# A recurrence, an attention mixture and a feed-forward block: norm's root on GpSimd, decay on ScalarE, mask as a VectorE copy

## The chip, the cores and the metric

The kernel runs on one core of one Trainium2 chip. The metric is device time in microseconds (us), the median over several executions. The core's engines run side by side, each with its own queue of instructions in a fixed order: TensorE (PE; its weight loads are PEld), VectorE (DVE), ScalarE (ACT), GpSimd (POOL) and SyncE (SP), which issues the transfers. An instruction waits until what it needs is done, and everything behind it in its queue waits with it.

## The reference

Three steps follow each other, each on the result of the one before. Sizes: 4 sequences (b), 768 steps, 8 heads of 48 columns (384 together), 4 experts of width 64, a feed-forward width of 1536.

```python
# 1. recurrence over time, a 48x48 state for each of 8 heads
for t in range(S):
    cur = einsum('bhd,bhe->bhde', u[None] * kt, vt)
    y[:, :, t] = einsum('bhd,bhde->bhe', rt, state + cur)
    state = wt[:, :, :, None] * state + einsum('bhd,bhe->bhde', kt, vt)
# 2. four causal attention experts, of which each row takes its top 2
logits = x @ w_gate; w = softmax over the top 2
q = x @ wq[e]; k = x @ wk[e]; v = x @ wv[e]
a = softmax(where(causal, -1e9, scale * (q @ k.T)))
out += mask * w * (a @ v @ wo[e])
# 3. norm and feed-forward, with the input added
xn = (x - mu) / sqrt(var + 1e-06) * g_ln
return x + maximum(xn @ w_ch1, 0.0) @ w_ch2
```

## The kernel before, in words

**Recurrence.** It is cut into 24 chunks of 128 steps, six to a sequence; `rwkv_chunk(n)` builds the work of one. Time lies along the free axis, four pairs of heads side by side, so the tiles are 128x512. Two scans on VectorE multiply up the decays (`scan` writes bw, `forth` writes fw), from bw also come the whole decay of the chunk (`decay`) and `begin`. k times bw is k2 (VectorE, `mk_k2`), r times fw is rp (GpSimd, `mk_rp`). TensorE multiplies them for each head (`mm_a`, into two PSUM banks pa, one for the even and one for the odd heads). This product is wanted only where the time of k lies before that of r: `am_copy` copies a bank to SBUF on ScalarE, and `am_mask` sets the rest to zero on GpSimd. `mm_intra` multiplies the masked tile am with v. What earlier chunks left behind is the state, a 48x48 block for each head: `mk_dec` multiplies it on GpSimd with the chunk's decay and writes it into a block-diagonal tile dec (two heads on the diagonal, zeros beside them), `mm_inter` multiplies that with rp into the same bank py, `mm_d` makes what the chunk adds, and `state` adds it to dec on VectorE and writes it into one of two tiles. k times r times u, summed by head, is done token by token on GpSimd and VectorE (`mk_rk`, `mk_ruk`, `mk_cb`, `mk_cv`); `xsum` adds it to py.

**Attention.** `project(b)` splits a sequence's rows into a high and a low half in fp16, transposes them by DMA and makes q, k, v and the gate. `attend(b)` goes over six tiles of 128 rows and four experts: scores ps, the row's maximum on VectorE (`s_max`, mx), the exponential on ScalarE (ex), the probabilities' high half on ScalarE and low half on GpSimd (hl), a transposing DMA (pt), the product with v (po), and the output projection (px, `mm_o`), which needs the low half o16 of VectorE.

**Norm and feed-forward.** For every two row tiles, `norm(b, g)` makes 1/sqrt of the variance from a bit trick (`n_start`, three instructions) and three Newton steps (`n_step`, four instructions each), all on VectorE on 128x2 elements, then normalises (`n_xn`, xn), splits (`n_hi`, `n_lo`) and transposes. `mlp(b, g)` runs the two products (pm and pz). Their weights come as raw integers and are decoded in the front part of the program, on VectorE (w_f), ScalarE and GpSimd (w_w).

**What sets the order.** Nothing is written in program order. Each step is an `op` with its engine, an assumed duration, what it comes after, and the buffers that it takes and frees. `Plan.order` then runs a list scheduler while the program is built: on each engine, of the steps that could start about now, it takes the one with the smallest due value, plus a price for lateness:

```python
o.due = sum(PLACE.get(k, 0.0) * f for k, f in o.terms)
...
pick = min(((o.due + late * (s - first), o.idx, s, o) for s, o in starts if s <= first + look))
```

PLACE is a table of some 270 numbers, one for each chunk, tile, group and kind of step; the order is fixed with it. While TensorE has nothing real to do, until 208 us of the planner's own time, it gets filler products of 128x512 (`spin`, line 577), whose results nobody reads.

## Time and profile before

| | |
|---|---|
| median of 3 runs | 743.48 us (739.04 to 746.66) |
| the profiled execution | 737.19 us, its span 735.3 |
| TensorE busy | 679.3 us, 92% of the span, 103.3 of it filler |
| VectorE busy | 518.8 us, 71% |
| ScalarE busy | 368.2 us, 50% |
| GpSimd busy | 295.3 us, 40% |

The span is that of the trace, from the first to the last instruction; 1.9 us lie around it. An average over the span says little here, since the program begins with recurrence, decoding and attention and ends with feed-forward.

### The profile page before, as it was taken

What the parts mean: (1) busy time and instruction counts of PE and PEld (TensorE: products, weight loads), DVE (VectorE), ACT (ScalarE), POOL (GpSimd) and SP (SyncE); (2) the same over time, 40 slices, a digit from 0 to 9 for tenths busy, and PEclk for the clock granted to TensorE, in tenths of its full rate; (3) what the DMA queues carried; (4) which work ended last, traced back from release to release, by engine and by line L of the source; (5) the groups of instructions that cost most, each with busy time, mean ns of one, the idle gap of its engine ahead of it and who ended that gap; (6) DMA issues with size and microseconds to landing.
All of it is one profiled execution on the core that took longest, in us unless ns stands there. A gap on an engine that the chain in (4) does not pass through costs nothing.

```text
span 735.3 us, 15608 instructions
## 1 busy us (share of the span) xinstructions
PE 679.3 (92%) x5753; PEld 486.6 (66%) x5753; DVE 518.8 (71%) x1326; ACT 368.2 (50%) x991; POOL 295.3 (40%) x317
## 2 busy tenths in 40 slices
PE   7899879998979899988999999989999989999996
PEld 4565536645557567766757686767677667685773
DVE  5888688787688996868899487957655754475521
ACT  5533473445867463556647445644553452554210
POOL 7366465444846671366546015650330220223000
PEclk9999889999989999999999999999999999999999
DMA  7555556736556684547695448464555342355110
GB/s 248 172 176 169 177 135 175 242 92 152 128 114 120 175 187 116 113 102 194 150 204 108 107 104 179 85 122 95 105 100 121 73 72 66 70 87 105 29 43 26
DMA packets 174004, 92.60 MB, mean 126 GB/s; under 512 B 144608, under 2 KB 156640, under 8 KB 173920
## 3 DMA queue, kind: packets, MB, share of 16 engines
q1 hardware_dynamic: 173920, 91.53, 53.3%
q8 instruction: 47, 0.77, 0.4%
q14 instruction: 37, 0.30, 0.1%
HBM read 44.31 MB, written 4.72 MB: 67 GB/s over the span
## 4 chain that ended last, share of the span: by engine, by line
PE 35%; DVE 26%; DMA 12%; ACT 6%; issue 4%; POOL 3%; SPq 1%; POOLq 0%; ACTq 0%; DVEq 0%
PE pz L1252 9%; DMA pt<-hl 9%; PE pm L1219 8%; PE pq L862 5%; DVE mx L1019 4%; POOL hl L1044 3%; PE py L757 2%; ACT ex L1031 2%; PE pv L917 2%; DMA xT<-xs 2%; DVE mx L1021 2%; DVE hid L1234 2%; PE spin L577 2%; DVE bw L631 1%; DVE fw L643 1%
## 5 line engine op out<-in xcount | busy, mean ns | idle before, releaser
L1044 POOL TENSOR_TENSOR hl<-ex,hl 128x128 f16<-128x128 f32 (+5 forms) x96 | 103.9, 1086 | 250.9 <-ACT hl L1040 207.9
L1219 PE MATMUL pm<-xnT,w_w 128*128 128x256 f16 x1296 | 154.6, 273 | 2.0 <-DVE hid L1234 1.3
L1252 PE MATMUL pz<-w_w,hid 128*128 128x384 f16 x864 | 153.1, 327 | 1.4 <-DVE hid L1234 1.4
L1219 PEld LDWEIGHTS <-w_w 128*128 128x128 f16 x1296 | 123.7, 98 | 20.3 <-issue 1.7
L1252 PEld LDWEIGHTS <-hid 128*128 128x128 f16 x864 | 82.1, 98 | 50.3 <-issue 1.4
L1031 ACT ACTIVATE ex<-ps,bias,scales 128x512 f32<-128x512 f32 (+3 forms) x128 | 79.9, 627 | 65.2 <-DVE bias L1023 51.6
L577 PE MATMUL spin<-starts,ident 128*128 128x512 bf16 x395 | 103.3, 403 | 2.9 <-POOL ident masks.py:199 2.1
L1019 DVE TENSOR_REDUCE mx<-ps 128x1 f32<-128x512 f32 (+3 forms) x128 | 61.4, 500 | 30.3 <-PE ps L1009 23.0
L577 PEld LDWEIGHTS <-ident 128*128 128x128 bf16 x395 | 39.1, 104 | 45.4 <-issue 10.9
L1230 ACT ACTIVATE hid<-pm 128x512 f16<-128x512 f32 x72 | 42.7, 593 | 52.6 <-PE pm L1219 52.5
L1040 ACT ACTIVATE hl<-ex 128x128 f16<-128x128 f32 (+5 forms) x96 | 54.4, 572 | 28.1 <-DMA pt<-hl 25.3
L1234 DVE SCALAR_TENSOR_TENSOR hid<-pm,hid 128x512 f16<-128x512 f32 x72 | 49.1, 683 | 21.9 <-ACT hid L1230 21.8
L1064 PE MATMUL po<-vt,pt 128*128 128x64 f16 x1008 | 45.3, 194 | 18.1 <-DMA pt<-hl 17.8
L1064 PEld LDWEIGHTS <-pt 128*128 128x128 f16 x1008 | 39.6, 99 | 31.9 <-DMA pt<-hl 27.1
L724 POOL TENSOR_SCALAR_AFFINE_SELECT am<-am 128x512 f32<-128x512 f32 x48 | 36.1, 767 | 49.0 <-ACT am L719 48.9
L862 PE MATMUL pq<-xT,w_qk 128*128 128x384 f16 x288 | 48.9, 326 | 1.5 <-DVE qk L881 1.5
L757 PE MATMUL py<-seq,am 128*128 128x48 f32 x384 | 46.7, 275 | 2.1 <-POOL am L724 2.1
L757 PEld LDWEIGHTS py<-seq,am 128*128 128x128 f32 x384 | 46.1, 194 | 3.5 <-POOL am L724 2.2
L667 POOL TENSOR_TENSOR rp<-seq,fw 128x512 f32<-128x512 f32 x24 | 32.4, 1351 | 27.4 <-DVE fw L643 22.2
L1006 PE MATMUL ps<-kd,qs 128*128 128x512 f16 (+3 forms) x128 | 39.7, 312 | 3.5 <-ACT ex L1031 3.4
L862 PEld LDWEIGHTS <-w_qk 128*128 128x128 f16 x288 | 28.0, 98 | 19.7 <-issue 2.0
L1007 PE MATMUL ps<-low,qs 128*128 128x512 f16 (+3 forms) x128 | 37.6, 312 | 0.0
(182 smaller groups left out, 1141.6 us busy)
## 6 DMA issues: line engine op xcount, KB each, us to landing
seq<-in_seq_dram SPq DMA_DIRECT2D x48, 256.0 KB, 4.2
tok<-in_tok_dram SPq DMA_DIRECT2D x24, 384.0 KB, 3.6
w_raw<-in_w_dram SPq DMA_DIRECT2D x36, 256.0 KB, 3.0
seq<-in_seq_dram SPq DMA_DIRECT2D x24, 258.5 KB, 3.0
...
```

What stands on the lines that cost most here:

```text
L577: T.matmul(bank("m", "spin"), ident16, ballast, start=True, stop=True)
L757: T.matmul(t["py"][:, h * D : (h + 1) * D], t["am"][h % 2][:, h // 2, :], t["vt"][:, h * D : (h + 1) * D], start=(c == 0 and h == 0), stop ...
L862: T.matmul(h["pq", half][:, :384].rearrange("p (c t) -> p c t", t=P), wt["qk"][:, lw, kk, mt * P : (mt + 1) * P], t["xT"][:, 3 * half : 3 ...
L1019: V.tensor_reduce(out=mx[:, ip : ip + 1], in_=h["ps"][ip][:, : k1 - k0], axis=AX.X, op=OP.max)
L1031: A.activation(h["ex"][:, k0:k1], h["ps"][ip][:, : k1 - k0], AF.Exp, bias=h["bias"], scale=t["esc"], accum_out=r["sums"][:, e, ip : ip + 1])
L1040: A.activation(h["hl"][:, :W], h["ex"][:, :W], AF.Copy)
L1044: G.tensor_tensor(out=h["hl"][:, W : 2 * W], in0=h["ex"][:, :W], in1=h["hl"][:, :W], op=OP.subtract)
L1064: T.matmul(r["po"][:, e * HD : (e + 1) * HD], r["pt"][e][:, lp * (i + 1) + kb, :], t["vt"][:, kb, lv, e * HD : (e + 1) * HD], start=(e == ...
L1219: T.matmul(h["pm"][:, j * 256 : (j + 1) * 256].rearrange("p (c t) -> p c t", t=P), wt["w1"][:, lw, kk, f * P : (f + 1) * P], q["xnT"][:, : ...
L1230: A.activation(hid[fp][:, 0], h["pm"], AF.Relu)
L1234: V.scalar_tensor_tensor(out=hid[fp][:, 1], in0=h["pm"], scalar=0.0, in1=hid[fp][:, 0], op0=OP.max, op1=OP.subtract)
L1252: T.matmul(h["po"][:, :DM], hid[fp][:, lh, c0 : c0 + P], wt["w2"][:, lw, 2 * fp + j, :], start=(fp + j + i == 0), stop=(fp == NF // 2 - 1 ...
```

## The change

Three steps are done in another way, and the table of the order is new.

- **Mask.** The copy to SBUF and the masking become one VectorE instruction, a copy under a mask (`copy_predicated`, with the 0/1 tile `above`). It writes only where the mask is 1; elsewhere the target keeps the zeros that it was given at the start. So the two targets (`ams`) are now fixed tiles, one for the even and one for the odd heads, and no longer taken from a ring.
- **Decay.** `mk_dec` moves from GpSimd to ScalarE, as four scaled copies of 128x96, one for each pair of heads, from one of the two block-diagonal tiles (`decs`) into the other. The state lives in these tiles: `state` adds into the tile in place. It must therefore wait for `mm_inter`, which reads the same tile, and `mm_d` is queued behind `mm_inter`.
- **Norm.** In place of `n_start` and three `n_step` stand one VectorE instruction (variance plus 1e-6, divided by 64) and one GpSimd instruction, that to the power -0.5.
- **Order.** The numbers of PLACE are all new, with the entries of the dropped steps left out.

```diff
--- before.py
+++ after.py
@@ -36,58 +36,57 @@
 
 PRM = dict(LOOK=0.09, LATE=389.29, UNTIL=208.0, SPAN=9.92, LEAST=2.644, GAP=0.05, NPA=6, NSM=0, NWA=24, NK2=0)
 PLACE = {
-    ('av', 0, 0): 2115.89, ('av', 0, 1): -962.38, ('av', 0, 2): -717.4, ('av', 0, 3): 4212.33, ('av', 0, 4): -1403.95,
...
+    ('av', 0, 0): -1586.12, ('av', 0, 1): -4443.5, ('av', 0, 2): -4729.91, ('av', 0, 3): 1027.27,
...
 }
 
 
@@ -277,7 +276,7 @@
     pass
 
 
-SIZES = dict(seq=2, bw=1, fw=2, rp=2, k2=2, tok=1, cv=1, dec=2, am=2, k2t=1, xf=1, xT=1, xs=2, qs=1, kd=1, kl=1,
+SIZES = dict(seq=2, bw=1, fw=2, rp=2, k2=2, tok=1, cv=1, am=2, k2t=1, xf=1, xT=1, xs=2, qs=1, kd=1, kl=1,
              vt=1, ex=2, hl=2, pt=3, of=1, o16=2, oT=2, hid=9, x1=3, xnT=2, r=3, a=2, o=1, m=2)
 RW = 256
 
@@ -339,12 +338,19 @@
     G.memset(neg, 0.0)
     G.affine_select(out=neg, in_=neg, compare_op=OP.is_ge, fill=-(2.0 ** 100), base=0,
                     pattern=[[-1, P]], channel_multiplier=1)
+    above = const.tile([P, P], mybir.dt.int8, name="above")
+    G.memset(above, 1)
+    G.affine_select(out=above, in_=above, compare_op=OP.is_ge, fill=0, base=-1, pattern=[[1, P]], channel_multiplier=-1)
+    ams = [const.tile([P, NP, P], F32, name=f"am{j}") for j in range(2)]
+    for a in ams:
+        V.memset(a, 0.0)
     begin = const.tile([P, NP * CW], F32, name="begin")
     V.memset(begin, 0.0)
-    states = [const.tile([P, NP, D], F32, name=f"state{i}") for i in range(2)]
     decs = [const.tile([P, NP, 2 * D], F32, name=f"dec{i}") for i in range(2)]
     for t in decs:
         V.memset(t, 0.0)
+    half = const.tile([P, 2], F32, name="half")
+    G.memset(half, -0.5)
     tri = const.tile([P, E, E], F32, name="tri")
     V.memset(tri, 0.0)
     for e in range(1, E):
@@ -693,13 +699,10 @@
 
         mk_dec = None
         if c:
-            @op("G", 0.94, after=[forth, before.get("state")], take=[mine("dec")])
+            @op("A", 1.18, after=[forth, before.get("state")])
             def mk_dec():
-                t["dec"] = decs[(b * (NC - 1) + c) % 2]
-                for j in range(2):
-                    rows, cols = slice(64 * j, 64 * j + D), slice(j * D, (j + 1) * D)
-                    G.tensor_tensor(out=t["dec"][rows, :, cols], in0=states[(c - 1) % 2][rows],
-                                    in1=decay[rows, n, :, None].to_broadcast([D, NP, D]), op=OP.mult)
+                for hp in range(NP):
+                    A.activation(decs[c % 2][:, hp], decs[(c - 1) % 2][:, hp], AF.Copy, scale=decay[:, n, hp : hp + 1])
 
         @op("PE", 1.0, dense=0.64, after=[mk_k2, mk_rp], follow=[before.get("py")], take=[mine(ta, 0), mine(ta, 1)], free=[mine("k2"), mine("rp")])
         def mm_a():
@@ -710,22 +713,15 @@
                     T.matmul(t["pa"][j][:, hp * P : (hp + 1) * P], t["k2"][o : o + D, hp, :], t["rp"][o : o + D, hp, :],
                              start=True, stop=True)
 
-        t["am"] = [None, None]
         masked = []
         for j in range(2):
-            @op("A", 0.59, after=[mm_a], follow=[me["am"] if j else before.get("am")], take=[mine("am", j)], free=[mine(ta, j)])
+            @op("V", 0.69, after=[mm_a], follow=[me["am"] if j else before.get("am")], take=[mine("am", j)], free=[mine(ta, j)])
             def am_copy(j=j):
-                t["am"][j] = buf("am", [P, NP, P], F32, f"am_{nm}_{j}")
-                A.activation(t["am"][j].rearrange("p h t -> p (h t)"), t["pa"][j], AF.Copy)
-
-            @op("G", 0.64, after=[am_copy])
-            def am_mask(j=j):
-                a = t["am"][j]
-                G.affine_select(out=a, in_=a, compare_op=OP.is_ge, fill=0.0, base=-1,
-                                pattern=[[0, NP], [1, P]], channel_multiplier=-1)
+                V.copy_predicated(ams[j], above[:, None, :].to_broadcast([P, NP, P]),
+                                  t["pa"][j].rearrange("p (h t) -> p h t", t=P))
 
             me["am"] = am_copy
-            masked.append(am_mask)
+            masked.append(am_copy)
 
         if not last:
             @op("PE", 0.44, after=[mk_k2], follow=[before.get("d")], take=[mine("r", "pk")], free=[mine("k2")])
@@ -741,11 +737,11 @@
 
         mm_inter = mm_d = None
         if c:
-            @op("PE", 0.9, dense=0.7, after=[mk_rp, mk_dec], follow=[mm_a], take=[mine("r", "py")], free=[mine("rp"), mine("dec")])
+            @op("PE", 0.9, dense=0.7, after=[mk_rp, mk_dec], follow=[mm_a], take=[mine("r", "py")], free=[mine("rp")])
             def mm_inter():
                 t["py"] = bank("r", f"py_{nm}")
                 for hp in range(NP):
-                    T.matmul(t["py"][:, hp * 2 * D : (hp + 1) * 2 * D], t["rp"][:, hp, :], t["dec"][:, hp, :],
+                    T.matmul(t["py"][:, hp * 2 * D : (hp + 1) * 2 * D], t["rp"][:, hp, :], decs[c % 2][:, hp, :],
                              start=(hp == 0), stop=False, skip_group_check=True)
 
         @op("PE", 1.74, dense=0.37, after=masked + [load_v], follow=[mm_inter], take=[] if c else [mine("r", "py")],
@@ -754,12 +750,12 @@
             if c == 0:
                 t["py"] = bank("r", f"py_{nm}")
             for h in range(H):
-                T.matmul(t["py"][:, h * D : (h + 1) * D], t["am"][h % 2][:, h // 2, :], t["vt"][:, h * D : (h + 1) * D],
+                T.matmul(t["py"][:, h * D : (h + 1) * D], ams[h % 2][:, h // 2, :], t["vt"][:, h * D : (h + 1) * D],
                          start=(c == 0 and h == 0), stop=(h == H - 1), skip_group_check=True)
 
         state = None
         if not last:
-            @op("PE", 0.79, dense=0.73, after=[mk_k2t, load_v], follow=[before.get("py")], take=[mine("r", "pd")], free=[mine("k2t"), mine("seq")])
+            @op("PE", 0.79, dense=0.73, after=[mk_k2t, load_v], follow=[mm_inter, before.get("py")], take=[mine("r", "pd")], free=[mine("k2t"), mine("seq")])
             def mm_d():
                 t["pd"] = bank("r", f"pd_{nm}")
                 for hp in range(NP):
@@ -767,16 +763,16 @@
                              t["vt"][:, hp * 2 * D : (hp + 1) * 2 * D],
                              start=(hp == 0), stop=(hp == NP - 1), skip_group_check=True)
 
-            @op("V", 0.72, after=[mm_d, mk_dec, before.get("dec")], free=[mine("r", "pd")] + ([mine("dec")] if c else []))
+            @op("V", 0.72, after=[mm_d, mm_inter, before.get("dec")], free=[mine("r", "pd")])
             def state():
                 pdv = t["pd"][:, :DM].rearrange("p (h j e) -> p h j e", j=2, e=D)
                 for j in range(2):
                     rows, cols = slice(64 * j, 64 * j + D), slice(j * D, (j + 1) * D)
-                    dst = states[c % 2][rows]
+                    dst = decs[c % 2][rows, :, cols]
                     if c == 0:
                         V.tensor_copy(dst, pdv[rows, :, j])
                     else:
-                        V.tensor_tensor(out=dst, in0=t["dec"][rows, :, cols], in1=pdv[rows, :, j], op=OP.add)
+                        V.tensor_tensor(out=dst, in0=dst, in1=pdv[rows, :, j], op=OP.add)
 
         @op("V", 0.56, after=[mm_intra, mk_cv], follow=[before.get("xsum")], take=[] if c else [("xf", b)],
             free=[mine("r", "py")])
@@ -1145,29 +1141,16 @@
         nm = f"{b}_{g}"
         plan.at("n", b, g)
 
-        @op("V", 0.5, after=att[b]["x1"][-2:])
-        def n_start():
-            q["v"], q["y"], q["t"] = (small(f"rs_{k}", [P, 2], f"rs_{k}_{nm}", 4) for k in "vyt")
-            V.tensor_scalar(q["v"], q["mv"][:, :, 1], 1e-6, None, op0=OP.add)
-            V.tensor_scalar(q["y"].bitcast(I32), q["v"].bitcast(I32), 1, None, op0=OP.logical_shift_right)
-            V.tensor_scalar(q["y"].bitcast(I32), q["y"].bitcast(I32), -1, 0x5F3759DF, op0=OP.mult, op1=OP.add)
-
-        step = n_start
-        for it in range(3):
-            @op("V", 0.65, after=[step])
-            def n_step(it=it):
-                v, y, t = q["v"], q["y"], q["t"]
-                V.tensor_tensor(out=t, in0=y, in1=y, op=OP.mult)
-                V.tensor_tensor(out=t, in0=t, in1=v, op=OP.mult)
-                V.tensor_scalar(t, t, -0.5, 1.5, op0=OP.mult, op1=OP.add)
-                if it < 2:
-                    V.tensor_tensor(out=y, in0=y, in1=t, op=OP.mult)
-                else:
-                    V.scalar_tensor_tensor(out=y, in0=y, scalar=8.0, in1=t, op0=OP.mult, op1=OP.mult)
-
-            step = n_step
-
-        @op("V", 0.87, pair=True, after=[step], take=[("ex", ("n", b, g))])
+        @op("V", 0.17, pair=True, after=att[b]["x1"][-2:])
+        def n_var():
+            q["v"], q["y"] = (small(f"rs_{k}", [P, 2], f"rs_{k}_{nm}", 4) for k in "vy")
+            V.tensor_scalar(q["v"], q["mv"][:, :, 1], 1e-6, 1.0 / 64, op0=OP.add, op1=OP.mult)
+
+        @op("G", 0.4, after=[n_var])
+        def n_root():
+            G.tensor_tensor(out=q["y"], in0=q["v"], in1=half, op=OP.pow)
+
+        @op("V", 0.87, pair=True, after=[n_root], take=[("ex", ("n", b, g))])
         def n_xn():
             q["xn"] = buf("ex", [P, 2, DM], F32, f"xn_{nm}")
             for t in range(2):
@@ -1277,8 +1260,8 @@
         seqs, toks = (a.rearrange("(b c) p n -> b c p n", c=NC) for a in (seq, tok))
         pair = small("pair", [P, 2], "pair", 1)
         G.memset(pair, 0.0)
-        state = states[0]
-        G.memset(state, 0.0)
+        state = decs[0][:, :, :D]
+        G.memset(decs[0], 0.0)
         for j in range(2):
             G.memset(pair[64 * j : 64 * j + 64, j : j + 1], 1.0)
         xf[B] = (buf("xf", [P, NC, DM], F32, "xf_g"), small("xm", [P, NC], "xm_g", 2))
```

The order moves in many places. Three are shown; in a row stand the line, the operation, what is written and what is read (names end in sequence, tile or chunk, and a running number).

VectorE ahead of the first norm's normalisation (rs_ are the Newton tiles, bw_2_0 is the scan of a chunk of sequence 2, xn the normalised rows), before:

```order
L1153 TENSOR_SCALAR rs_y_0_0_2625<-rs_y_0_0_2625 128x2
L1160 TENSOR_TENSOR rs_t_0_0_2626<-rs_y_0_0_2625 128x2
...
L1162 TENSOR_SCALAR rs_t_0_0_2626<-rs_t_0_0_2626 128x2
L1166 SCALAR_TENSOR_TENSOR rs_y_0_0_2625<-rs_y_0_0_2625,rs_t_0_0_2626 128x2
L631 SCALAR_TENSOR_TENSOR bw_2_0_2660<-seq_2_0_2588,starts_69 128x516
L1174 TENSOR_SCALAR xn_0_0_2712<-x1_0_0_2408,mv_0_0_2409,rs_y_0_0_2625 128x384 x2
L1019 TENSOR_REDUCE mx_0_3_1_2716<-ps_0_3_1_0_2703 128x1
```

The same place now (scales_1 and s_x1 belong to sequence 1's projection, am0 and am1 are the masked copies of chunk 2_0):

```order
L1147 TENSOR_SCALAR rs_v_0_0_2667<-mv_0_0_2576 128x2
L637 SCALAR_TENSOR_TENSOR bw_2_1_2670<-seq_2_1_2591,starts_69 128x516
...
L419 RECIPROCAL s_x1_2683<-inv_x1_2682 128x1
L809 TENSOR_SCALAR scales_1_2688<-inv_x1_2682 128x1
...
L814 COPY scales_1_2688<-s_x1_2683 128x1
L720 COPY_PREDICATED am0_91<-above_88,pa_2_0_0_2650 128x512
L720 COPY_PREDICATED am1_92<-above_88,pa_2_0_1_2651 128x512
L1157 TENSOR_SCALAR xn_0_0_2723<-x1_0_0_2575,mv_0_0_2576,rs_y_0_0_2668 128x384 x2
L1084 TENSOR_TENSOR of_0_2_2744<-po_0_2_2593,den_0_2_2551 128x256
```

The Newton rows are gone; between the variance and the normalisation now stand sequence 1's scale factors and a chunk's two masked copies, and the recurrence has reached chunk 2_1 where it had reached 2_0.

GpSimd around chunk 1_1 of the recurrence (tok and cv belong to r times k times u, w_w1 is the decoding of weights), before:

```order
L667 TENSOR_TENSOR rp_1_1_1422<-seq_1_1_1178,fw_1_1_1348 128x512
L701 TENSOR_TENSOR dec0_92<-state0_90,decay_109 48x4x48 x2
L564 TENSOR_TENSOR w_w1_117<-w1_f1_578,w_w1_117 128x512
L564 TENSOR_TENSOR w_w1_117<-w1_f8_1056,w_w1_117 128x512
L671 TENSOR_TENSOR tok_1_1_1239<-tok_1_1_1239 128x384
L724 AFFINE_SELECT am_1_1_0_1512<-am_1_1_0_1512 128x512
L724 AFFINE_SELECT am_1_1_1_1525<-am_1_1_1_1525 128x512
L681 TENSOR_TENSOR tok_1_1_1239<-tok_1_1_1239,u_sb_111 128x384
```

and now:

```order
L570 TENSOR_TENSOR w_w1_124<-w1_f7_1060,w_w1_124 128x512
L697 TENSOR_TENSOR cv_1_1_1451<-seq_1_1_1057,cb_1_1_1225 128x384
L673 TENSOR_TENSOR rp_1_1_1487<-seq_1_1_1057,fw_1_1_1227 128x512
L570 TENSOR_TENSOR w_w1_124<-w1_f4_825,w_w1_124 128x512
L570 TENSOR_TENSOR w_w1_124<-w1_f3_780,w_w1_124 128x512
L673 TENSOR_TENSOR rp_1_2_1533<-seq_1_2_1194,fw_1_2_1443 128x512
```

The masks and the products for dec are gone from this queue, and rp of the next chunk stands three rows behind that of this one.

VectorE around the scan of the last chunk, 3_5 (hid is the hidden layer of the feed-forward, the numbers behind it sequence and group), before:

```order
L1234 SCALAR_TENSOR_TENSOR hid_1_1_4_6750<-pm_1_1_4_6697,hid_1_1_4_6750 128x512
L1184 TENSOR_TENSOR x16_2_0_6878<-xn_2_0_6820,x16_2_0_6878 128x2x384
...
L631 SCALAR_TENSOR_TENSOR bw_3_5_6920<-seq_3_5_6861,starts_69 128x516
L637 RECIPROCAL begin_88<-bw_3_5_6920 128x4
L638 COPY decay_109<-bw_3_5_6920 128x4
L662 TENSOR_TENSOR k2_3_5_6941<-seq_3_5_6861,bw_3_5_6920 128x512
L643 SCALAR_TENSOR_TENSOR fw_3_5_6947<-seq_3_5_6861,begin_88 128x516
L1234 SCALAR_TENSOR_TENSOR hid_1_1_5_6943<-pm_1_1_5_6846,hid_1_1_5_6943 128x512
```

and now:

```order
L1217 SCALAR_TENSOR_TENSOR hid_0_2_2_5090<-pm_0_2_2_5044,hid_0_2_2_5090 128x512
L1015 TENSOR_REDUCE mx_1_4_0_5225<-ps_1_4_0_0_5157 128x1
...
L1167 TENSOR_TENSOR x16_1_0_5124<-xn_1_0_4994,x16_1_0_5124 128x2x384
L637 SCALAR_TENSOR_TENSOR bw_3_5_5263<-seq_3_5_5201,starts_69 128x516
L1217 SCALAR_TENSOR_TENSOR hid_0_2_3_5247<-pm_0_2_3_5191,hid_0_2_3_5247 128x512
L775 TENSOR_TENSOR dec1_98<-dec1_98,pd_3_3_5165 48x4x48 x2
L1217 SCALAR_TENSOR_TENSOR hid_0_2_4_5277<-pm_0_2_4_5237,hid_0_2_4_5277 128x512
```

The last scan stood beside the feed-forward of sequence 1's second group, and now stands beside that of sequence 0's last.

## Rows read from the trace of the kernel before

**Rows 1.** Windows: us from and to, length, busy us (count) of PE, PEld, DVE, ACT, POOL; PEclk, DMA, GB/s.

```profile
0.00:220.00 220.00, 195.00 (x1307) 123.06 (x1308) 172.05 (x413) 116.24 (x356) 121.71 (x142) 0.94 0.58 166
220.00:440.00 220.00, 205.69 (x1961) 156.82 (x1959) 177.13 (x453) 123.72 (x335) 103.70 (x105) 1.00 0.65 139
440.00:500.00 60.00, 55.02 (x521) 43.39 (x519) 45.05 (x115) 31.52 (x90) 32.90 (x39) 0.97 0.62 128
500.00:735.30 235.30, 223.60 (x1972) 163.30 (x1970) 124.58 (x347) 96.75 (x214) 36.98 (x32) 0.99 0.38 77
340.00:360.00 20.00, 17.07 (x194) 14.52 (x193) 19.34 (x48) 10.49 (x28) 11.71 (x12) 1.00 0.67 148
```

**Rows 2.** Windows, of the filler products of line 577 alone: busy us of PE and PEld.

```profile
0.00:220.00 220.00, 103.28 (x395) 39.13 (x395) 0.94 0.58 166
220.00:735.30 515.30, 0.00 (x0) 0.00 (x0) 0.99 0.52 109
```

**Rows 3.** Chain of waits, 196 to 225 us: shares by line, then start and length.

```profile
by line: DVE xn L1174 8.6%; DVE bw L631 7.5%; DVE mx L1019 7.0%; issue 6.9%; DVE xs L831 6.8%; DVE fw L643 5.8%; PE pd L766 5.1%; DVE rs_t L1161 4.1%; DVE rs_t L1160 4.1%; PE pk L735 3.8%; DVE st L1134 3.6%; DVE rs_t L1162 3.2%; PE spin L57
...
196.96 0.18 DVE rs_y L1152
...
202.17 0.16 DVE rs_y L1166
```

**Rows 4.** Waits, VectorE, 0 to 220 us: us in total, times, longest.

```profile
DVE w_f L481 <- DMA w_raw<-in_w_dram: 7.3, 6, 1.8
...
DVE xf L786 <- PE py L757: 6.1, 3, 3.3
```

**Rows 5.** Groups by line and shape, GpSimd, 0 to 220 us: busy us, mean ns, idle before.

```profile
L724 POOL TENSOR_SCALAR_AFFINE_SELECT am<-am 128x512 f32<-128x512 f32 x24 | 18.1, 763 | 20.1 <-ACT am L719 20.0
...
L701 POOL TENSOR_TENSOR dec<-state,decay 48x192 f32<-48x192 f32 x20 | 11.7, 583 | 1.7 <-DVE state L779 1.0
```

**Rows 6.** Groups by line and shape, the whole trace.

```profile
L757 PE MATMUL py<-seq,am 128*128 128x48 f32 x384 | 46.7, 275 | 2.1 <-POOL am L724 2.1
...
L631 DVE TENSOR_TENSOR_SCAN bw<-seq,starts 128x516 f32<-128x516 f32 x24 | 34.3, 1427 | 1.5 <-DMA seq<-in_seq_dram 1.5
...
L710 PE MATMUL pa<-rp,k 48*128 48x128 f32 x384 | 29.1, 290 | 3.2 <-DVE k L662 2.2 <-DVE state L779 1.0
...
L719 ACT ACTIVATE am<-pa 128x512 f32<-128x512 f32 x48 | 26.9, 588 | 13.0 <-PE pa L710 12.9
...
L748 PE MATMUL py<-dec,rp 128*128 128x96 f32 x160 | 21.5, 277 | 0.1
...
L662 DVE TENSOR_TENSOR k<-seq,bw 128x512 f32<-128x512 f32 x24 | 20.0, 835 | 3.2 <-DMA seq<-in_seq_dram 3.2
```

**Rows 7.** One line's instructions: ns at least/median/most, first and last start.

```profile
L631 DVE TENSOR_TENSOR_SCAN bw<-seq,starts x24: 1204/1226/2608, 3.6 to 480.5; 128x516 f32<-128x516 f32 x24
...
L1234 DVE SCALAR_TENSOR_TENSOR hid<-pm,hid x72: 659/683/693, 224.1 to 718.2; 128x512 f16<-128x512 f32 x72
```

**Rows 8.** Windows, the instructions that touch the Newton temporary rs_t: busy us of VectorE.

```profile
0.00:735.30 735.30, 30.65 (x144) 0.98 0.54 126
```

**Rows 9.** Groups by line and shape, GpSimd, the whole trace.

```profile
L564 POOL TENSOR_TENSOR w_w<-w_f,w_w 128x512 f16<-128x512 f32 x18 | 21.7, 1212 | 0.6 <-ACT w_w L561 0.4
...
L545 POOL TENSOR_SCALAR iout<-iout 128x1 f32<-128x1 f32 x1 | 0.2, 226 | 0.1
```

**Rows 10.** Groups by line and shape, ScalarE, the whole trace: scaled copies.

```profile
L463 ACT ACTIVATE w_qk<-raw_qk,s_small 128x256 f16<-128x256 f32 x6 | 2.5, 495 | 3.1 <-DVE s_small L413 3.1
...
L463 ACT ACTIVATE w_vg<-raw_vg,s_small 128x4 f16<-128x4 f32 x3 | 0.7, 282 | 0.0
```

**Rows 11.** Timeline: start, length, engine, line; TensorE at 219, VectorE at 316 us.

```profile
219.61 2.14 PE L1219 MATMUL pm<-xnT,w_w 128*128 128x256 f16 x18
...
316.66 0.55 DVE L1098 TENSOR_TENSOR o<-of,o 128x256 f16<-128x256 f32 x1 [0.40 <-ACT o L1094]
```

**Rows 12.** Waits, TensorE, 345 to 735 us: us in total, times, longest.

```profile
PE po L1064 <- DMA pt<-hl: 8.5, 9, 1.8
```

More of the change, by code (lines that the diff above doesn't have):

```diff
@@ L91 @@
+    's_hi': -129.58, 's_lo': -5161.82, 's_max': 1106.06, 's_tr': 814.87, 'scan': 744.0, 'se': -226.28,
+    'stack': 3292.82, 'state': 13424.5, 'times': 237.14, 'top': -290.94, 'unpack': -1844.73, 'v_hi': 770.61,
+    'v_lo': 548.42, 'vc': -234.31, 'w_check': 510.01, 'ws_hi': -3976.67, 'ws_lo': -628.77, 'ws_load': 1812.92,
+    'ws_top': 602.69, 'x_hi': 155.59, 'x_lo': 633.61, 'x_tr': -359.44, 'xabs': -941.24, 'xsum': -287.03,
 }
```

31 lines of the change are left out of this document (13 added, 18 removed), and 66 rows, old and new, of the table PLACE.

## The prediction

> **What bounds the kernel now.** I read the stretches first, then the spins, the chain of waits, the waits of VectorE, and last the prices by shape. In the stretches the reader is to see two different kernels [rows 1]. From 220 us on TensorE is busy 484.3 of 515.3 us, and nothing in it is filler [rows 2]. Up to 220 us it is busy 195.0 us, but 103.3 us of that are spins [rows 2], so real work fills only 92 us; the time goes into what feeds it. VectorE is the busiest of the feeders, 172.05 of 220 us (78%), with GpSimd at 121.71 and ScalarE at 116.24. The chain of waits says which of them it is: just ahead of the first feed-forward matmuls it runs mostly on VectorE, through the Newton steps of the first norm, the normalisation and a scan [rows 3]. VectorE's 48 us of idle time there are many short waits, the longest sums for weights still being loaded (7.3 us) and the masked product of the recurrence (6.1) [rows 4]. So the span is a front that VectorE sets, then TensorE work with some 31 us of holes: 14.3 in 220 to 440, 5.0 in 440 to 500 and 11.7 behind that.
>
> **The change, part by part.**
> *Mask.* A chunk loses two ScalarE copies (588 ns [rows 6]) and two GpSimd masks (763 ns in the front [rows 5]), and gets two masked VectorE copies of the same 128x512 from PSUM. The trace has no such copy. From below its bound is the VectorE instruction that reads 128x512 from PSUM with one SBUF operand, 683 ns, 659 at the least [rows 7]; from above the product of two SBUF operands of that size, 835 ns with its stalls; a form that takes as long as the scan, 1427 ns, is the far end [rows 6]. I take 0.683, the nearest in operands. That is 48 x 0.683 = 32.8 us more on VectorE, 26.9 less on ScalarE and 48 x 0.763 = 36.6 less on GpSimd. A chunk's masked product then waits for one engine instead of two in a row.
> *Norm.* Per group of two tiles, 14 of 15 small VectorE instructions go, since the first one stays with another constant. The 144 that touch the Newton temporary take 30.65 us [rows 8], 0.213 each; the other 24 (shift, multiply) at the same price add 5.1: 35.8 us over 12 norms. The first norm's took from 196.96 to 202.33, 5.4 us [rows 3], more than 15 x 0.213 = 3.2. In their place GpSimd raises 128x2 elements to a power: above 0.23 us (its one-column instruction) and, unless it is slower than a whole 128x512 subtraction, below 1.21 us [rows 9]. I take 0.4 and two handovers; at either end it is less than what goes, and 12 x 1.21 = 14.5 us would be hidden on an engine that loses 36.6 and 23.3 in the other two parts. What is queued behind it on GpSimd are the probabilities' low halves, which mostly wait for ScalarE.
> *Decay.* 40 GpSimd products of 583 ns in the front (23.3 us [rows 5]) become 20 x 4 scaled ScalarE copies of 128x96. Six scaled copies of 128x256 were busy 2.5 us, so 0.42 each back to back; one of 128x4 took 0.28 [rows 10]. The values between give some 0.3, so 1.2 us a chunk, 24 us in all, against the 26.9 us that ScalarE loses: nothing, and ScalarE is not the bound in any stretch. In exchange the new state is added into the tile that the product with r reads, so a chunk's state must wait for that product, about 1.1 us of TensorE (21.5 us over 20 chunks [rows 6]). The front runs two sequences' recurrences, 12 chunks in 220 us, some 18 us for each, so I cost this at nothing; if the chain of states ever sets the pace, it costs 1.1 us a chunk.
> Over the whole span VectorE loses 3 us, ScalarE 3, GpSimd 55 (60 less 12 x 0.4), TensorE only the 20 spins that the new order leaves out (5.2 us of filler, no time in itself).
>
> *Where it lands* matters more. Up to the low half of the first norm the new order puts on VectorE 26 masked copies (17.8 us), one more pair of scans (2 x 1.43 [rows 6]) with its row reduction and sum (about 1.0), two more state copies (0.7) and the scale factors of batch 1 (about 2.2); it takes off the Newton steps (5.4) and a maximum (0.9). Sum: **18 us more VectorE work in the front**. Against it stands contention. The backward scan takes 1.23 us at the median and up to 2.61, while the instruction with one PSUM operand never leaves 659 to 693 ns [rows 7]; the gap is about one GpSimd instruction long. A scan's mean lies 0.2 us above its median [rows 6, 7], 2.6 us over the 13 that stand in the front. The forward scans beside them, the products, the decoding of weights and the Newton steps stretch as well; I estimate 15 us in the front for all of them. GpSimd loses there 18.1 + 11.7 of 121.7 us [rows 1, 5], a quarter: 4 us back. So 172 us become 186.
> On this the Trainium skill (SBUF — State Buffer, Who interferes with whom) says that a VectorE instruction with at most one SBUF input does not contend with GpSimd, and one with two does. The trace agrees, 72 instances in 659 to 693 ns [rows 7]. By that rule the copy costs 0.683 and gains from the emptier GpSimd; if it reads its own destination as a second input, the 0.835 of the product holds, 7.3 us more in all and 4 more in the front.
> If VectorE idled as before (48 us) the front would take 234 us. For 220 us its idle time must fall to 34 us, 15% instead of 22%. That can be: a queue with more ready work in it waits less for a load or a product that comes meanwhile, the wait of 6.1 us stood behind two engines and now stands behind one, and in 340 to 360 VectorE was busy 19.34 of 20 us [rows 1]. I take 15%, so **the front gives -1 us**.
> The next place is the output projection of batch 1's first tile, whose low half VectorE writes at 316.66 us [rows 11]. Up to there, by the mean of the stretches, it was busy 172.05 + 0.805 x 97 = 250 of 317 us (21% idle). The new order runs the recurrence ahead: four more chunks' scans and 40 masked copies stand in front, minus three norms' steps, 41 us in all; less 5 for contention that is 286. TensorE's queue has more in front as well: five chunks' first products (29.1 / 24 = 1.21 a chunk) and masked ones (46.7 / 24 = 1.95) [rows 6], with small change some 22 us, less 5.2 of spins. So it stays even at 317 + 17 = 334 us, with 14% idle. The same share decides, and I count nothing.
> *Behind 317 us* the last recurrences are out of the way: before, the last scan began at 480.5 us [rows 7], and in 440 to 500 TensorE stood for 5.0 us. In the new order they are through while the feed-forward of batch 0's last group runs. The waits there are for transposed probabilities (8.5 us from 345 on [rows 12]), behind a GpSimd and a VectorE that now have less to do. I count **-4 us**, of the 5.0.
>
> **Sum.** 735.3 - 1 - 4 = 730.3 us of span, 732.2 with the 1.9 that lie around it in the profiled execution (737.19). The median of the runs shown, 743.48, lies 6.3 above that execution, so I forecast **738.5 us**. Runs of one kernel spread over 1%, so within 1% (736.0 to 750.9) a measurement can hardly tell it from no change.
>
> **Rivals.**
> *The dense VectorE really runs dense.* In 220 to 440 it was busy 177.13 of 220 us (80%) while TensorE was the bound; alone in 340 to 360 it reached 97% [rows 1]. If its idle share falls to 10%, the front is 186 / 0.9 = 207 us, 13 less, and with the 4 behind that is 718 + 1.9 + 6.3, **726 us**. For it: short chains, free GpSimd. Against: the 7.3 us for weights being loaded [rows 4] stay.
> *VectorE becomes the bound and idles as before.* Its in-order queue now carries the masked copies, and each waits for a product of TensorE; behind it stand scans, the maxima of scores and the low halves. Kept at 22% idle the front takes 186 / 0.78 = 238 us, 18 more, and the second place would come later as well. With the 4 given back: 735.3 + 18 - 4 + 8.2, **757.5 us**. It decides from 15% idle on: each point above costs 2.5 us. For it: on the chain in the front VectorE was bound already, and still idled 22%.
> *The copy isn't what it says.* At 1.43 us, as the scan, 26 copies cost 19 us more in the front, with the same 757 us; at 0.835, 4 us. I put this into the chance of the one above.
>
> **How the numbers follow.** Forecast 0.42, faster rival 0.31, slower one 0.27. The forecast's own range is 731 to 748 (12% to 18% idle). The range reaches to both rivals' values and a little beyond, 724 to 759. Faster by over 1% takes the first rival and the lower edge of the forecast, 0.35; within 1% 0.40; slower 0.25.
>
> **What would show it.** Masked copies near 0.68 us with a narrow spread; the power at 0.2 to 1.2 us; the decay near 1.2 us a chunk. VectorE about 186 us busy when the first feed-forward matmul starts, and this start within 8 us of 219.6 [rows 11]. TensorE's holes from 440 us on smaller than the 16.7 us of before. The forecast is wrong if that start moves by over 10 us, or if holes open in the middle, where VectorE's lead is now shorter.

## The result, and the profile after

The changed kernel takes **719.85 us** (median of 4 runs, 718.12 to 721.62) against 742.91 in the same comparison: ratio 0.969, 95% interval 0.9635 to 0.9746. That is 18.7 us under the forecast and 4 us under the low end of its range.

The windows of the changed kernel, cut as before and at its first feed-forward matmul (columns as in [rows 1]):

```profile
0.00:207.85 207.85, 184.79 (x1277) 118.69 (x1281) 176.43 (x425) 113.97 (x376) 99.18 (x108) 0.95 0.62 177
207.85:718.10 510.25, 483.78 (x4453) 363.67 (x4453) 322.87 (x784) 251.42 (x648) 144.44 (x137) 0.99 0.53 110
...
220.00:440.00 220.00, 206.59 (x1955) 159.53 (x1954) 169.89 (x406) 122.42 (x356) 83.58 (x76) 0.98 0.64 142
440.00:500.00 60.00, 58.36 (x548) 43.92 (x547) 37.64 (x106) 33.78 (x84) 14.67 (x18) 1.00 0.54 99
500.00:718.10 218.10, 207.01 (x1835) 150.26 (x1832) 106.00 (x254) 87.44 (x193) 38.95 (x36) 1.00 0.38 74
```

The same cut of the kernel before, at its own first feed-forward matmul:

```profile
0.00:219.61 219.61, 194.62 (x1303) 122.70 (x1304) 171.73 (x411) 115.85 (x355) 121.71 (x142) 0.94 0.58 166
219.61:735.30 515.69, 484.69 (x4452) 363.87 (x4450) 347.09 (x917) 252.37 (x637) 173.57 (x175) 0.99 0.52 109
```

The spins of the changed kernel (line 583 there), busy us of PE and PEld:

```profile
0.00:207.85 207.85, 91.90 (x371) 36.74 (x375) 0.95 0.62 177
```

Read them in this order. The first feed-forward matmul starts at 207.85 us in place of 219.61 [rows 11], 11.8 us sooner. By then TensorE has done 184.79 - 91.90 = 92.9 us of real work, before it was 194.62 - 103.28 = 91.3, so the same front is done in less time. Behind that point TensorE is busy equally long (483.78 and 484.69) and stands for 26.5 us in place of 31.0. So of the 17.2 us between the two spans **11.8 come from the front and 5.4 from behind it**, 4.5 of these as smaller holes. The two medians lie 23.1 us apart, more than the spans, because the profiled execution before (737.19) was shorter than most of its kind (medians of 740.5 to 742.9 in four comparisons), while the changed kernel's (720.01) lies at its median. No trace of a typical execution of the kernel before was taken, so where these 6 us lie stays open.

VectorE in the front does more than before (176.43 us against 171.73) in less time: its idle share fell from 21.8% to 15.1%. Its waits there, in the changed kernel (us in total, times, longest):

```profile
DVE cb L692 <- POOL tok L687: 7.4, 6, 3.5
DVE den L1077 <- ACT ex L1027: 5.9, 1, 5.9
DVE w_f L487 <- DMA w_raw<-in_w_dram: 2.5, 3, 1.1
...
DVE am L720 <- PE py L753: 2.3, 1, 2.3
...
DVE xf L782 <- PE py L753: 0.2, 1, 0.2
```

The wait for the masked product has gone from 6.1 to 0.2 us and that for weights from 7.3 to 2.5 [rows 4]. One wait of 2.3 us is new: a masked copy had to wait until TensorE had read the fixed tile of the chunk before. The new instructions, line by line (ns at least/median/most, first and last start):

```profile
L720 DVE COPY_PREDICATED am<-above,pa x48: 700/722/744, 11.2 to 385.0; 128x512 f32<-128x512 int8 x48
...
L1151 POOL TENSOR_TENSOR rs_y<-rs_v,half x12: 688/691/1572, 195.4 to 670.7; 128x2 f32<-128x2 f32 x12
...
L705 ACT ACTIVATE dec<-dec,decay x80: 357/360/376, 13.6 to 385.2; 128x96 f32<-128x96 f32 x80
```

### The profile page after: what moved, and what is told of

Read it like the earlier page. It is cut to its first block, busy times and chain, and to the rows that moved or that the text cites. A ratio compares the mean times of both kernels' runs of the same rounds, so it can differ in the third digit from the quotient of the medians.

```text
span 718.1 us, 15387 instructions
## 1 busy us (share of the span) xinstructions
PE 668.6 (93%) x5729; PEld 482.4 (67%) x5733; DVE 499.3 (70%) x1208; ACT 365.4 (51%) x1023; POOL 243.6 (34%) x244
## 4 chain that ended last, share of the span: by engine, by line
PE 38%; DMA 15%; DVE 13%; ACT 3%; issue 3%; POOL 3%; SPq 1%; ACTq 0%; POOLq 0%; DVEq 0%
PE pm L1202 11%; PE pz L1235 11%; DMA pt<-hl 9%; PE pq L858 4%; PE po L1060 3%; PE px L1112 2%; DVE mx L1015 2%; POOL hl L1040 2%; PE pv L913 2%; DMA oT<-o 1%; DMA tok<-in_tok_dram 1%; PE spin L583 1%; DMA seq<-in_seq_dram 1%; DVE am L720 1%; DVE hid L1217 1%
## 5 line engine op out<-in xcount | busy, mean ns | idle before, releaser
L1040 POOL TENSOR_TENSOR hl<-ex,hl 128x384 f16<-128x384 f32 (+5 forms) x96 | 102.3, 1069 | 261.1 <-ACT hl L1036 223.5
L1202 PEld LDWEIGHTS <-w_w 128*128 128x128 f16 x1296 | 125.4, 98 | 19.9 <-issue 1.9
L583 PE MATMUL spin<-starts,ident 128*128 128x512 bf16 x371 | 91.9, 394 | 2.3 <-POOL ident masks.py:199 2.1
L1015 DVE TENSOR_REDUCE mx<-ps 128x1 f32<-128x512 f32 (+3 forms) x128 | 61.3, 499 | 22.6 <-PE ps L1005 11.4
L1036 ACT ACTIVATE hl<-ex 128x384 f16<-128x384 f32 (+5 forms) x96 | 54.7, 573 | 30.4 <-DMA pt<-hl 24.2
L583 PEld LDWEIGHTS <-ident 128*128 128x128 bf16 x375 | 36.7, 101 | 43.8 <-issue 6.3
L1060 PEld LDWEIGHTS <-pt 128*128 128x128 f16 x1008 | 37.2, 98 | 19.8 <-DMA pt<-hl 15.5
L1060 PE MATMUL po<-vt,pt 128*128 128x64 f16 x1008 | 41.4, 193 | 9.1 <-DMA pt<-hl 8.9
L858 PEld LDWEIGHTS <-w_qk 128*128 128x128 f16 x288 | 28.0, 98 | 20.9 <-issue 3.6
L658 ACT ACTIVATE seq<-seq 128x128 f32<-128x128 f32 x96 | 28.4, 298 | 23.9 <-DVE fw L649 21.8
L677 POOL TENSOR_TENSOR tok<-tok 128x384 f32<-128x384 f32 x24 | 26.2, 1090 | 36.4 <-DMA tok<-in_tok_dram 36.4
```

Source lines behind the costliest of these rows:

```text
L583: T.matmul(bank("m", "spin"), ident16, ballast, start=True, stop=True)
L858: T.matmul(h["pq", half][:, :384].rearrange("p (c t) -> p c t", t=P), wt["qk"][:, lw, kk, mt * P : (mt + 1) * P], t["xT"][:, 3 * half : 3 ...
L1015: V.tensor_reduce(out=mx[:, ip : ip + 1], in_=h["ps"][ip][:, : k1 - k0], axis=AX.X, op=OP.max)
L1036: A.activation(h["hl"][:, :W], h["ex"][:, :W], AF.Copy)
L1040: G.tensor_tensor(out=h["hl"][:, W : 2 * W], in0=h["ex"][:, :W], in1=h["hl"][:, :W], op=OP.subtract)
L1060: T.matmul(r["po"][:, e * HD : (e + 1) * HD], r["pt"][e][:, lp * (i + 1) + kb, :], t["vt"][:, kb, lv, e * HD : (e + 1) * HD], start=(e == ...
```

## The experiments

Three theories stood against each other. **Parts**: the new steps free VectorE and GpSimd, in whichever order. **Order**: the new table brings the gain. **Both**: each pays only with the other. In all of them but e12 only what a step issues is changed; the planner sees the same durations, so each engine's queue keeps its order around the step. In e12 it makes an order of its own. e1, e5 and e7 keep the changed kernel's tiles, so the state stays in `decs` and `mm_d` behind `mm_inter`. All were timed beside the kernel before (740.5 to 741.2 us in these comparisons). The table's columns from "first" on come from each profiled execution, cut at the first feed-forward matmul as above; "holes" is TensorE's idle time behind it. A profiled execution can lie some us off the median beside it (e3's took 729.5, e7's 723.4, e10's 765.6).

| | median us | ratio to before, interval | first us | VectorE busy till then, idle share | TensorE busy behind, holes |
|---|---|---|---|---|---|
| before | 742.91 | 1 | 219.6 | 171.7, 21.8% | 484.7, 31.0 |
| changed | 719.85 | 0.969 (0.9635 to 0.9746) | 207.9 | 176.4, 15.1% | 483.8, 26.5 |
| e1 new order, old steps | 767.9 | 1.040 (1.031 to 1.049) | 223.2 | 172.8, 22.6% | 494.7, 47.1 |
| e2 old order, new mask and norm | 740.1 | 1.001 (0.997 to 1.005) | 219.9 | 175.8, 20.1% | 489.0, 28.2 |
| e3 old order, new norm | 734.0 | 0.992 (0.988 to 0.996) | 217.8 | 169.1, 22.4% | 485.4, 24.6 |
| e4 changed, dead GpSimd masks | 724.9 | 0.979 (0.972 to 0.986) | 212.1 | 181.7, 14.4% | 484.1, 27.9 |
| e5 changed, old mask | 738.2 | 0.995 (0.991 to 0.998) | 215.7 | 164.2, 23.9% | 487.5, 34.2 |
| e6 changed, old norm | 751.0 | 1.014 (1.008 to 1.020) | 216.1 | 180.1, 16.7% | 494.6, 38.0 |
| e7 changed, old decay | 726.2 | 0.982 (0.976 to 0.987) | 212.0 | 179.0, 15.6% | 481.7, 27.9 |
| e8 changed, copies twice | 754.1 | 1.018 (1.012 to 1.023) | 228.8 | 193.5, 15.4% | 492.9, 30.4 |
| e9 changed, more ScalarE | 725.9 | 0.981 (0.974 to 0.988) | 214.4 | 177.0, 17.4% | 481.3, 26.7 |
| e10 before, more VectorE | 762.9 | 1.028 (1.022 to 1.035) | 236.3 | 184.0, 22.1% | 489.7, 37.8 |
| e11 changed, half copies | 718.6 | 0.967 (0.959 to 0.975) | 206.9 | 170.4, 17.6% | 483.9, 25.6 |
| e12 before, new table | 768.0 | 1.036 (1.029 to 1.042) | 233.4 | 170.9, 26.7% | 495.8, 39.2 |

**e1, e2, e3 and e12: steps against order.**

```diff
 # e1, in the changed kernel (decay and norm likewise)
-                V.copy_predicated(ams[j], above..., t["pa"][j]...)
+                A.activation(ams[j]..., t["pa"][j], AF.Copy)
+                G.affine_select(out=ams[j], in_=ams[j], ...)
 # e2 in the kernel before; e3 has the second part alone
-                A.activation(t["am"][j]..., t["pa"][j], AF.Copy)
+                V.copy_predicated(ams[j], above..., t["pa"][j]...)
...
+            V.tensor_scalar(q["v"], q["mv"][:, :, 1], 1e-6, 1.0 / 64, op0=OP.add, op1=OP.mult)
+            G.tensor_tensor(out=q["y"], in0=q["v"], in1=half, op=OP.pow)
 # e12 in the kernel before: all numbers of PLACE from the changed kernel
```

> All three steps are done as before the change (ScalarE copy and GpSimd mask, GpSimd decay, Newton steps on VectorE), each issued at the place of the new step in the new order; TensorE's and SyncE's order is that of the changed kernel to the row. Theory 'parts' (the new steps themselves free VectorE and GpSimd, in whichever order): the gain of 23 us goes, 738 to 748 us. Theory 'order' (the new table brings the gain, the steps hardly matter): it stays, 718 to 727 us. Theory 'both' (the order pays only with the steps that it was made for): slower than the kernel before, over 750 us.

> The kernel before in its old order, with the masked copy in the place of the ScalarE copy and the power in the place of the first Newton step; the decay stays on GpSimd with the state in tiles of its own. Theory 'parts': most of the gain is here, 722 to 733 us. Theory 'order': 738 to 748 us, as before. Theory 'both': 738 us or more, since VectorE's old queue now carries 26 copies more ahead of the first feed-forward.

> The kernel before in its old order, with the power alone in the place of the Newton steps. VectorE loses 36 us over the trace, 5 of them ahead of the first feed-forward. Theory 'parts': 5 us in front and 2 to 3 behind, 734 to 738 us. Theories 'order' and 'both': within 3 us of the kernel before.

> The kernel before with the new table of numbers (the first and the further Newton steps take the numbers of variance and power, the mask has none), so that the scheduler makes its own order from the old durations by the new numbers, and the issue positions fit the old steps. Theory 'the gain is the new steps with an order that fits them': no better than before, 738 us or more. Theory 'the table is better for any steps': under 732 us.

"Both" holds in the main. The new order with the old steps is 4.0% slower than before, and the new table with a schedule of its own for the old steps 3.6% slower, so in neither form does the order pay by itself. The new mask and norm in the old order change nothing, which fits "order" as well as "both". The norm alone gives 0.8% there (6.5 us), as "parts" had it and against "both", so the masked copies take back what the norm gives. In e1 the waits of TensorE show where the old steps miss (us in total, times, longest):

```profile
PE py L756 <- POOL am L723: 10.8, 14, 1.2
PE po L1063 <- DMA pt<-hl: 10.5, 17, 2.2
PE py L747 <- POOL dec L706: 7.5, 9, 2.3
```

Two of the three lines are GpSimd's masks and GpSimd's decay, which the new order no longer leaves time for (before, TensorE stood 2.1 us for the masks and 0.1 ahead of the decay's product [rows 6]).

**e4: contention.**

```diff
+                G.affine_select(out=dead, in_=dead, ...)   # 128x384, beside each masked copy
```

> The changed kernel; beside each masked copy GpSimd also masks a tile of 128x384 that nobody reads, which gives it back most of the work that it lost (48 x about 0.6 us) without anyone waiting for the result. Theory 'contention' (VectorE's front became shorter because GpSimd stands less in its way, 7.6 us by the prices of its rows): the first feed-forward comes 3 to 5 us later and the kernel takes 723 to 726 us. Theory 'no contention' (fewer handovers and a fuller queue did it): within 2 us of the changed kernel's 720.

The windows of e4, and its masks by line:

```profile
0.00:212.12 212.12, 185.54 (x1280) 118.44 (x1280) 181.66 (x427) 114.76 (x378) 117.20 (x134) 0.95 0.60 173
```

```profile
L724 POOL TENSOR_SCALAR_AFFINE_SELECT dead<-dead 128x384 f32<-128x384 f32 x48 | 28.9, 602 | 0.9
```

Nobody waits for these masks, yet 18.0 us more of GpSimd in the front (117.20 against 99.18) put 5.2 us more on VectorE (181.66 against 176.43), 0.38 of them the memset of the tile. The first feed-forward comes 4.3 us later, and the kernel takes 5.0 us more. Both lie in the ranges of "contention". So this GpSimd work costs VectorE 4.85 / 18.0 = 0.27 us per us here.

**e5, e6 and e7: one old step each, in the new order.**

```diff
 # e6 (e5: the mask lines of e1; e7: two G.tensor_tensor products for the four A.activation)
-            G.tensor_tensor(out=q["y"], in0=q["v"], in1=half, op=OP.pow)
+            V.tensor_scalar(...)   # shift, multiply, then three Newton steps on VectorE
```

> The changed kernel in its new order, only the mask as before: a ScalarE copy and a GpSimd mask at the place of each masked copy. If the mask carries the change (TensorE waited 10.8 us for masked tiles and VectorE longer for GpSimd with all three steps old): 740 to 755 us, first feed-forward at 213 us or later. If it is one of three like parts: 728 to 738 us. If the mask costs nothing on its own, as VectorE then loses 32 us of copies: within 5 us of 720.

> The changed kernel in its new order, only the norm as before: the shift, the multiply and three Newton steps on VectorE at the place of the power. VectorE gets 14 instructions in each norm, some 3 us, 5 in the first. If VectorE's queue sets the front: first feed-forward 3 to 5 us later, in all 723 to 730 us. If the power's handovers cost as much as the steps: within 2 us of 720.

> The changed kernel in its new order, only the decay as before: two GpSimd products at the place of the four scaled ScalarE copies. If the decay is free where it stands, as I costed it: within 2 us of 720. If GpSimd's queue delays it (TensorE waited 7.5 us for it with all three steps old) and GpSimd stretches VectorE: 724 to 732 us.

Against the changed kernel's 719.85, mask 18 us, norm 31, decay 6: all three are needed, and the norm most, far over my 3 to 10. (The mask's 738.2 lies between its two ranges; the decay's 726.2 is in the range of "GpSimd's queue".) Of e5's waits, GpSimd's in the whole trace, then VectorE's in the front:

```profile
POOL am L721 <- ACT am L720: 53.6, 26, 5.6
```

```profile
DVE cb L692 <- POOL tok L687: 15.3, 8, 4.1
DVE dec L776 <- PE pd L763: 8.4, 4, 4.3
```

With the old mask GpSimd stands 53.6 us for ScalarE's copies, and r*k*u is queued behind; VectorE waits 15.3 us in the front for that product, in place of 7.4, and 8.4 in place of 0.9 for the product that makes the new state. VectorE's work in the front is 12.2 us less than in the changed kernel, but it idles 51.5 us in place of 31.4 (23.9% in place of 15.1%): the handovers cost more than the copies. In e6 VectorE is busy 26.4 us longer over the trace (525.7 against 499.3) and the span is 30.6 us longer: 8.3 in the front, 11.5 more holes behind it, and 10.8 because the same matmuls there take 494.6 us in place of 483.8. Stretches of e6, the first all that lies behind its first feed-forward matmul, then of the changed kernel (the column behind POOL is TensorE's granted clock):

```profile
216.11:748.70 532.59, 494.60 (x4455) 370.59 (x4452) 345.55 (x936) 250.49 (x646) 133.52 (x124) 0.97 0.50 104
200.00:250.00 50.00, 43.73 (x402) 34.00 (x402) 43.94 (x105) 27.82 (x82) 21.23 (x19) 0.93 0.70 155
250.00:300.00 50.00, 48.43 (x440) 36.81 (x440) 42.53 (x88) 28.14 (x95) 23.48 (x20) 0.94 0.73 169
300.00:350.00 50.00, 43.43 (x401) 33.38 (x398) 39.11 (x125) 26.05 (x75) 15.30 (x20) 1.00 0.56 121
350.00:400.00 50.00, 45.00 (x397) 36.91 (x396) 41.57 (x105) 25.35 (x77) 19.33 (x17) 0.86 0.64 139
...
354.80:358.80 4.00, 1.14 (x10) 0.99 (x9) 3.50 (x16) 0.52 (x1) 0.00 (x0) 1.00 1.38 291
358.80:369.00 10.20, 9.80 (x52) 7.85 (x52) 5.51 (x13) 4.74 (x12) 6.01 (x6) 0.50 0.67 139
```

```profile
200.00:250.00 50.00, 47.48 (x463) 37.26 (x463) 45.50 (x95) 31.86 (x97) 26.04 (x22) 1.00 0.81 178
250.00:300.00 50.00, 47.19 (x446) 36.06 (x445) 41.56 (x92) 26.19 (x90) 20.17 (x18) 1.00 0.78 193
300.00:350.00 50.00, 45.47 (x393) 34.00 (x391) 35.97 (x106) 29.60 (x77) 18.34 (x23) 0.93 0.58 113
350.00:400.00 50.00, 45.70 (x461) 36.81 (x462) 42.72 (x101) 29.57 (x86) 23.87 (x20) 1.00 0.60 129
```

In three of the four stretches of 50 us the clock granted in e6 is 0.86 to 0.94, where the changed kernel has 1.00; from 300 to 350 it is the other way round. Over all that lies behind the first feed-forward it is 0.97 against 0.99. That is some 16 us of clock lost against 5, an estimate from these rounded shares, and the difference is about the 10.8 us. One fall in detail: in the 4 us ahead of 358.8 TensorE was busy for 1.14 us, and then the granted clock was 0.50 (the lower of its two levels, 1.2 GHz) for 10.2 us, in which TensorE was busy for 9.80.

**e8, e9, e10 and e11: what time on a queue costs.**

```diff
 # e8                                   # e11: rows of half of the heads only
+                V.copy_predicated(ams[j], above..., t["pa"][j]...)   # once more
 # e9
+                A.activation(dead, t["pa"][j][:, : 3 * P], AF.Copy)
 # e10, in the kernel before
+                V.tensor_reduce(out=dead, in_=t["pa"][j]..., axis=AX.X, op=OP.max)
```

> The changed kernel with each masked copy done twice, 48 copies more on VectorE, 26 of them ahead of the first feed-forward; a pair took 1.20 us, so 0.6 each at the least and 0.72 at the most. If VectorE's work sets the front one to one: 15 to 19 us later there, 735 to 742 us in all. If the 15% in which VectorE is idle take it up: less than 6 us, under 726.

> The changed kernel; beside each masked copy ScalarE also copies 128x384 of the same bank to a tile that nobody reads, 48 x about 0.5 us. The doubled VectorE copies (30.2 us more busy VectorE) cost 34 us. Theory 'VectorE' (its queue sets the pace, the others follow): under 7 us more than 720. Theory 'tight order' (time added on any queue of an order made for other durations costs about itself): 15 us more or over.

> The kernel before with 48 more VectorE instructions, a row maximum over each 128x512 bank of the recurrence's first product, at the place of its ScalarE copy, 0.68 us each, 33 us in all. Theory 'VectorE' (bound by VectorE in the old order too): 765 to 778 us. Theory 'the old order has slack on VectorE' (taking 36 us of Newton steps away gave it only 6.5): under 755 us.

> The changed kernel with masked copies of the first half of each bank only, so that the masked product of half of the heads is left out of the result; VectorE loses some 48 x 0.27 = 13 us. Theory 'VectorE' one to one in both directions: 705 to 710 us. Theory 'tight order' (lost time costs, gained time is not used): 715 to 720 us.

Time added to VectorE costs itself or more: in e8 30.2 us more busy VectorE (529.5 against 499.3) cost 34.3, 12 us over the range expected. Some 21 of them lie in the front and 13 behind it, 9 of these because TensorE is busy 492.9 us in place of 483.8 there. In the old order of e10 the added instructions take 32.9 us (29.6, if each counts until the next one starts) and the others 8.3 less, so that VectorE is busy 21.3 us longer (540.1 against 518.8). The median is 21.7 us longer, between the two ranges expected, the span of the profiled execution 28.5. VectorE also stood for ScalarE's copy ahead of the added instructions:

```profile
DVE dead L721 <- ACT am L720: 17.0, 20, 3.8
```

So e10 added a wait together with the work, and does not tell the two apart. Copies on ScalarE in the same place (48 x 487 ns = 23.4 us) cost 6. Time taken from VectorE is not used: in e11 it loses 13.8 us (485.5 against 499.3) and the kernel 1.3, less than this comparison can tell from nothing. So in the new order theory "VectorE" is right for added time and wrong for removed time; "tight order" is wrong for ScalarE. The window of e8's front:

```profile
0.00:228.80 228.80, 200.52 (x1280) 127.18 (x1281) 193.51 (x452) 114.25 (x377) 104.86 (x110) 0.90 0.57 162
```

VectorE has 17.1 us more in it (193.51 against 176.43), and the first feed-forward comes 20.9 us later, at an idle share of 15.4% against 15.1%.

## Why the prediction was wrong, point by point

The forecast was 18.7 us too high. Of these, 10.8 are the front (-1 forecast, -11.8 measured), 1.4 the part behind it (-4 and -5.4), and 6.5 the last step of the sum.

**The failed step is the term "18 us more VectorE work in the front", less 4 for contention**, which put 186 us of VectorE before the first feed-forward. It was 176.4. The idle share behind it came out as forecast, 15% and 15.1%, so in the prediction's own terms the work was mis-sized. I counted the front's VectorE time row by row in both traces, each instruction until the next one starts, so that overlaps count once; a row that stands in one trace more often is priced at its mean before. The difference of 4.7 us (176.43 - 171.73) consists of four terms:

| term | forecast | measured |
|---|---|---|
| masked copies | +17.8 | +16.2 |
| Newton steps gone | -5.4 | -4.8 |
| more instructions (scans, factors, memsets) | +5.9 | +4.3 |
| the same instructions, cheaper | -4 | -11.0 |

The largest miss is contention. GpSimd lost 22.5 us in the front (121.71 to 99.18), and by e4's 0.27 that is 6 us of VectorE; I took a quarter of an estimated 15. What made the other 5 us cheaper is not shown by a run of its own. A smaller miss is the place up to which I counted the moved work, the first norm's low half. The timelines before show it, and a short operation that gained too (start, length; the two normalisations, the low half, then GpSimd beside the normalisations):

```profile
203.39 2.48 DVE L1174 TENSOR_SCALAR xn<-x,mv,rs_y 128x384 f32<-128x384 f32 x2
...
208.89 0.95 DVE L1184 TENSOR_TENSOR x<-xn,x 128x768 f16<-128x768 f32 x1
```

```profile
203.24 1.19 POOL L1044 TENSOR_TENSOR hl<-ex,hl 128x512 f16<-128x512 f32 x1 [2.51 <-ACT hl L1040]
204.39 2.50 POOL L564 TENSOR_TENSOR w_w<-w_f,w_w 128x512 f16<-128x512 f32 x2
```

and the same two places in the changed kernel:

```profile
199.11 0.86 DVE L1157 TENSOR_SCALAR xn<-x,mv,rs_y 128x384 f32<-128x384 f32 x2
...
202.62 0.95 DVE L1167 TENSOR_TENSOR x<-xn,x 128x768 f16<-128x768 f32 x1
```

From the end of the low half to the first feed-forward matmul it is 9.8 us before (209.84 to 219.61) and 4.3 after (203.57 to 207.85). VectorE's work in these 9.8 us belonged to the front of before, and I had left it out of the comparison. The two normalisations take 0.86 us where they took 2.48. Of the 24 in the trace before, 21 take 0.47 to 0.48 us; the other three take 1.25 to 1.31, began early in a GpSimd instruction, and ended 0.22 us after it did. The changed kernel has five that began beside a GpSimd instruction with over 0.3 us to go, each ending again 0.22 us behind the end of the GpSimd instruction. One of the eight, from the trace before:

```profile
475.20 1.31 DVE L1174 TENSOR_SCALAR xn<-x,mv,rs_y 128x384 f32<-128x384 f32 x1
```

```profile
474.93 1.37 POOL L1044 TENSOR_TENSOR hl<-ex,hl 128x512 f16<-128x512 f32 x1 [1.99 <-ACT hl L1040]
```

So an instruction with one tensor from SBUF can also be held up by GpSimd, which my list of contending forms did not have.

**How far this account carries.** 176.43 / 0.849 = 207.85 is how the share is defined, and no proof that VectorE's work sets the front. e11 took 6.0 us of VectorE out of the front, which came only 0.9 us sooner while the idle share rose to 17.6%; e9 left VectorE's work as it was, and the share rose to 17.4%. The share is not fixed, as the quotient had it: added work moved the front, removed work did not. So it stays open how much of the 11.8 us the cheaper work would have brought in another order.

**The last step of the sum failed too**: the 6.3 us by which the median before lay above the profiled execution were carried over to the changed kernel. Its median lies 0.2 us below its profiled execution.

**Idle share, 15%: right in size, the reason right in part.** Of the 16.5 us less idle time (47.9 and 31.4) the named wait for the masked product brought 5.9, less the new 2.3, and that for weights 4.8; waits for r*k*u grew (4.5 to 7.4). e5 shows that the mask's two handovers would keep the share at 24% in this order, and e2 that the old order makes little use of their going: 20.1%. To hit 15.1% was luck as well, since the share was a choice between 10 and 22%.

**Middle, "I count nothing": right in size.** Holes in 220 to 440 are 13.4 us, before 14.3. The output projection of batch 1's first tile got its low half at 328.0 us with 275.9 us of VectorE work, where I had 334 and 286.

**Behind, -4: right.** Holes from 440 us on are 12.7 us (1.64 + 11.09) against 16.7.

**Prices.** The copy takes 722 ns (0.683 taken), within 44 ns. The Trainium skill's rule (SBUF — State Buffer, Who interferes with whom) has a condition that I had left out: at most one SBUF input doesn't contend with GpSimd outside the 2-port modes of VectorE. For the copy the trace agrees: with the mask from SBUF it takes 700 to 744 ns, and 711 to 744 in the 17 of 48 that began while GpSimd was running, so GpSimd does not hold it up as it does the normalisations. The power 691 ns where I took 0.4, hidden in all but 2.8 us. The decay is busy 23.3 us (24 forecast).

**Newton steps.** I weighed them by what stands ahead of the two places, and gave those behind no term of their own. In the old order that was about right: without them (e3) the span behind the first feed-forward is 5.7 us shorter, 7.5 in all. In the new order the norm's 26 us of VectorE cost 31 (e6), most of it behind the first feed-forward. Over the whole span VectorE lost 19.5 us (518.8 to 499.3), not 3.

**Rivals.** The dense one was near in time (726, its front 207) but by another mechanism, which is luck: its 207 is 186 us at 10% idle, and neither came about. That VectorE idles as before is what e1 (22.6%) does, not the change. The copy is what it says.

**What stays open**: which moves in the new table make it fit the new steps. e1, e2 and e12 show that neither half works alone in the forms tried; they don't single out a move. Nor does any run have the old steps in an order made anew for them, so how much of the gain a better order alone could have brought is not shown. e2 also lacks the new decay, which could not be put into the old order, since there TensorE's state product stands ahead of the product that reads the old state.
